# A hand-ordered attention and gated-MLP kernel: whole K copies, an earlier flag read, two separate output tiles and another order of units

## The chip, the core and the metric

The kernel runs on one core of a Trainium2 chip. A core has a matrix engine (TensorE, PE in the profile, with its weight loads shown apart as PEld), a vector engine (VectorE, DVE), a scalar engine (ScalarE, ACT), a general engine (GpSimd, POOL) and a queue engine that only issues transfers (SyncE, SP). Each engine works through its own list of instructions in order and waits on semaphores for the others. Matrix products are written to PSUM, a small memory that the vector and scalar engines read; all other data lies in SBUF. The metric is the time of one execution in microseconds of device time, and lower is better.

## The reference, cut to what matters

For 4 batches of 8 heads, 768 positions and head width 64, the kernel computes an attention within blocks whose keys and values are first mixed over the 8 blocks by a matrix P, and then a gated MLP with a mixing over positions:

```python
P = sort_net                                   # [4, 8, 8, 8]
for _ in range(5):
    P = exp(P - max(P, -1))
    P = P / (sum(P, -1) + 1e-9)
    P = P / (sum(P, -2) + 1e-9)
k_sorted = einsum('bhij,bhjcd->bhicd', P, k_b)  # blocks of 96 positions
v_sorted = einsum('bhij,bhjcd->bhicd', P, v_b)
attn = softmax(q_b @ k_sorted^T / 8)            # within each block
x = (attn @ v_sorted) as [4, 768, 512]

h = maximum(x @ w_in, 0); u, v = halves of h    # 512 each
v_n = (v - mean(v)) / sqrt(var(v) + 1e-6)
v_s = einsum('ts,bsd->btd', w_spatial, v_n) + b_spatial
out = (u * v_s) @ w_out                         # [4, 768, 512], float32
```

## The kernel before, in words

The whole program is a hand-written list of units, the string `ORDER` (lines 18 to 48). A loop at line 692 reads it word by word and calls the function of that name (`SC:1:0:3:0` calls `u_SC(1, 0, 3, 0)`), which emits its instructions on its engines. The place of a word is therefore the place of its instructions in the list of every engine that it uses. A tile framework adds the waits that the data need. A unit's first number, where it has products, is one of four PSUM tiles (`ps_tile`, line 102), each of two banks; a letter A, D or P names the engine that copies (ACT, DVE or POOL). The framework lets two engines read one PSUM tile only one after the other.

Start. `S0` loads the sort net on SP's queue, `SK:0` to `SK:4` (line 223) are five rounds of normalisation, each with one exponential on ACT and six small operations on DVE; they leave P transposed. `MC` (line 210) makes a spread identity, `MA` and `MB` a mask; `DM` (line 216) are products on zeros that keep PE busy meanwhile. `PR` multiplies P and the spread identity into PSUM. `P0` (line 260) multiplies mask and that PSUM tile into the mixing matrices of batch 0, on DVE, two heads at a time. `PC` (line 269) copies P from PSUM to SBUF, and `PD` (line 272) makes the mixing matrices of the later batches from the copy, on POOL.

Loads. All inputs but the sort net and the bias `b_bc` are loaded on POOL's queue by `L` (line 156), converted to bfloat16 in flight. They land one after the other in the order of their words. A load waits until one of eight semaphores is free, and the tiles of q, k, v and the two halves of `w_spatial` share eight buffers. `BI` (line 187) loads the bias, spread over 128 partitions, on SP's queue.

Attention, by batch, pair of heads `hp` and half of the blocks `ih`. `QT` and `QQ` transpose q for one or two pairs. `KT` (line 370) mixes and transposes k and copies the result to SBUF; the helper `natural` (line 292) splits that copy between engines when its engine word has two letters (`DA`, `AD`: the first half on the first engine). `VT` and `VB` do the same for v of batch 0; for later batches `VM` mixes v into `vm` and `VC` (line 400) moves it to `vb` by eight copies on SP's queue. `SC` (line 414) multiplies scores, with an exponential on ACT into one of five `ex` tiles; `AT` (line 459) multiplies by v, with a reciprocal and a product on DVE. `XT` transposes the result by products; batches 2 and 3 use `XD` (line 482), two DMA transposes on SP's queue.

MLP, by batch. `VP` multiplies and rectifies the v half (one or two row tiles of 128); `ST`, `LN` and `LA` are its LayerNorm on DVE and ACT; `UP` makes the u half. `WT` transposes `w_spatial` once. `SP` (line 564) mixes positions with 12 products and adds the bias on DVE into `z`, of which there are two buffers; `GT` multiplies by u, on DVE or POOL. `OP` (line 588) multiplies by `w_out` for two row tiles of 128 rows into the two banks of one PSUM tile; with two more numbers it does only some of the four terms of the sum. `OE` (line 602) copies to `o_sb`, of which there are two buffers, and `OS` (line 608) stores on SP's queue; with two more numbers they take one of the two row tiles.

Range check. The main path leaves out the maxima of the reference. `CK` (line 617) tests on DVE whether the sums that were met are in range, `CF` adds the marks with one small product, and `LF` (line 638) reads the flag into a register of every engine; after the list a branch (line 696) goes to `general_path` if it is set. It isn't set with these inputs. In the list before, `CK` stands behind batch 3's last gating product, and `CF:2 LF` are the last words.

The last words before, from the last mixing on, are:

```
SP:3:3:3 OP:1:3:0:0:3 GT:D:3:3
OP:0:3:4:0:3 OP:-1:3:0:3:4 OE:A:3:0:1:2 OP:3:3:2:0:3 CK OS:2:4 OP:-1:3:2:3:4 OE:D:3:2:1:2 OE:A:3:0:0:1 OP:-1:3:4:3:4
OS:3:0:1:2 OS:3:0:0:1 OE:A:3:2:0:1 OS:3:2:0:1 OS:3:2:1:2 OE:A:3:4:0:1 OS:3:4:0:1 OE:A:3:4:1:2 OS:3:4:1:2 CF:2 LF
```

Of the kernel before, what the change touches and what calls it, by code (L numbers as in the profile page):

```python
# [15 lines left out]


ORDER = """
S0 CO SK:0 L:q:0:0:8 L:k:0:0:8 L:v:0:0:8 L:v:1:0:8 BH SK:1 SK:2 L:k:1:0:8 ID IV:2 MC IV:0 DM:1:6:512 L:q:1:0:8 SK:3
L:wv MA DM:3:6:512 DM:1:6:512 DM:2:6:512 SK:4 L:wsb QT:1:A:0:0 MB QT:0:D:0:1 QT:3:A:0:2 DM:2:6:512 PR:3 DM:2:6:512  # L20
P0:0:2 KT:1:A:0:0 P0:6:8 L:wu P0:4:6 PC:D P0:2:4 PD:1:0:4 QT:0:D:0:3 L:wsa IV:1 PD:1:4:8 KT:2:DA:0:1 KT:3:DA:0:3
SC:1:0:0:0 SC:0:0:1:1 KT:2:D:0:2 SC:3:0:0:1 L:q:2:0:8 VT:1:D:0:0 SC:0:0:2:0 L:k:2:0:8 VT:2:D:0:1 SC:3:0:3:1 VB:1:D:0:0
VT:0:A:0:2 VB:2:D:0:1 VT:3:A:0:3 AT:1:0:0:1 VB:0:A:0:2 L:v:2:0:8 AT:2:0:0:0 L:wo VB:3:D:0:3 PD:3:0:4 SC:1:0:3:0
AT:0:0:1:1 SC:2:0:1:0 SC:3:0:2:1 AT:1:0:3:1 VM:2:A:1:0 AT:0:0:1:0 VM:3:A:1:1 AT:1:0:2:1 VM:2:A:1:2 XT:0:D:0:1:0
KT:3:A:1:2 AT:1:0:2:0 KT:0:A:1:0 AT:2:0:3:0 XT:3:A:0:1:2 KT:0:A:1:3 QQ:1:D:1:0 VM:2:A:1:3 XT:0:D:0:0:2 XT:3:D:0:0:0
SC:1:1:0:0 QQ:2:D:1:2 VC:1:0:4 KT:0:A:1:1 VP:1:D:0:0:1 SC:3:1:2:1 ST:0:0 SC:0:1:3:1 VP:2:A:0:4:5 WT:3:A:5 WT:1:D:4
VP:0:A:0:3 ST:0:5 PD:2:0:4 SC:2:1:1:0 ST:0:3 SC:1:1:2:0 UP:3:A:0:1:0 VP:2:A:0:2 VC:1:4:8 ST:0:1 ST:0:4 AT:0:1:0:0
ST:0:2 WT:1:A:3 SC:3:1:3:0 LN:0:0:6 UP:2:A:0:0:1 AT:0:1:2:0 AT:1:1:3:0 LA:0:0 PD:2:4:8 UP:3:A:0:1:1 WT:0:D:0 LA:0:2
LA:0:1 LA:0:4 AT:2:1:2:1 LA:0:3 XT:1:A:1:0:2 LA:0:5 L:v:3:0:8 WT:3:A:1 UP:0:A:0:0:0 WT:3:D:2 BI SC:1:1:0:1 QQ:2:A:2:2
AT:3:1:1:0 AT:0:1:3:1 SP:1:0:3 SC:2:1:1:1 XT:0:D:1:1:2 XT:3:A:1:0:0 AT:1:1:0:1 AT:2:1:1:1 SP:0:0:2 XT:2:A:1:1:0  # L30
GT:P:0:3 KT:1:AD:2:3 KT:3:AD:2:2 KT:0:DA:2:0 KT:2:A:2:1 GT:P:0:2 QQ:1:A:2:0 SC:0:2:3:0 VM:3:D:2:3 SP:2:0:1 VM:1:A:2:2
VM:0:A:2:1 VP:3:D:1:0:1 VM:2:A:2:0 SP:1:0:0 SC:0:2:2:1 SC:2:2:1:1 GT:P:0:1 VC:2:4:8 VC:2:0:4 ST:1:1 VP:3:A:1:4:5
SC:1:2:1:0 SC:0:2:3:1 GT:P:0:0 UP:2:A:1:0:0 PD:3:4:8 ST:1:0 ST:1:4 VP:3:D:1:2:3 VM:2:A:3:3 VM:1:A:3:0 OP:0:0:2 ST:1:2
OE:A:0:2 L:k:3:0:8 AT:1:2:3:1 VM:2:A:3:2 UP:3:A:1:1:0 ST:1:5 AT:0:2:2:1 ST:1:3 VM:2:D:3:1 L:q:3:0:8 UP:1:A:1:0:1
AT:3:2:1:1 LN:1:0:6 UP:0:A:1:1:1 LA:1:1 AT:1:2:3:0 OP:2:0:0 LA:1:0 SC:1:2:0:1 SC:0:2:2:0 OP:3:0:4 LA:1:5 OS:0:2
OE:D:0:0 LA:1:3 LA:1:4 LA:1:2 AT:2:2:0:1 AT:0:2:2:0 SP:1:1:0 OE:A:0:4 XD:2:1 SC:2:2:0:0 KT:0:DA:3:2 QQ:3:D:3:2
KT:1:D:3:1 KT:2:AD:3:0 SP:0:1:2 KT:2:A:3:3 OS:0:4 GT:D:1:0 QQ:1:A:3:0 AT:3:2:1:0 AT:0:2:0:0 VP:2:D:2:4:5 VC:3:0:4
VC:3:4:8 SC:3:3:3:0 SC:1:3:3:1 ST:2:4 XD:2:0 SP:0:1:1 SC:2:3:2:1 GT:D:1:2 SC:1:3:1:1 SP:3:1:3 AT:0:3:3:0 GT:P:1:3
AT:2:3:3:1 VP:1:A:2:2:3 ST:2:5 VP:0:A:2:0:1 OS:0:0 AT:1:3:2:1 GT:P:1:1 ST:2:3 UP:2:D:2:0:1 OP:1:1:2 SC:3:3:0:0
OE:D:1:2 ST:2:2 SC:2:3:1:0 UP:0:A:2:1:0 SC:1:3:0:1 ST:2:1 ST:2:0 LN:2:0:6 SC:3:3:2:0 UP:2:D:2:0:0 AT:0:3:1:1 LA:2:5  # L40
LA:2:4 LA:2:2 OS:1:2 UP:1:A:2:1:1 OP:2:1:0 AT:1:3:0:0 OE:A:1:0 LA:2:0 LA:2:3 LA:2:1 OP:3:1:4 AT:2:3:1:0 AT:0:3:2:0
SP:1:2:1 XD:3:0 AT:2:3:0:1 XD:3:1 GT:D:2:1 OE:A:1:4 SP:0:2:0 SP:1:2:3 GT:D:2:0 SP:0:2:2 OS:1:4 UP:3:D:3:0:0 OS:1:0
VP:0:D:3:2:3 GT:D:2:2 VP:1:A:3:0:1 ST:3:3 GT:D:2:3 ST:3:2 UP:3:A:3:0:1 VP:0:A:3:4:5 ST:3:1 OP:3:2:2 ST:3:0 OP:2:2:0
ST:3:5 ST:3:4 OE:A:2:2 LN:3:0:6 UP:1:A:3:1:1 LA:3:1 UP:0:A:3:1:0 LA:3:5 LA:3:3 LA:3:0 LA:3:2 OE:A:2:0 LA:3:4 SP:1:3:2
SP:3:3:0 GT:P:3:2 SP:0:3:1 OP:2:2:4 GT:D:3:1 OS:2:0 OS:2:2 OE:A:2:4 GT:D:3:0 SP:3:3:3 OP:1:3:0:0:3 GT:D:3:3
OP:0:3:4:0:3 OP:-1:3:0:3:4 OE:A:3:0:1:2 OP:3:3:2:0:3 CK OS:2:4 OP:-1:3:2:3:4 OE:D:3:2:1:2 OE:A:3:0:0:1 OP:-1:3:4:3:4
OS:3:0:1:2 OS:3:0:0:1 OE:A:3:2:0:1 OS:3:2:0:1 OS:3:2:1:2 OE:A:3:4:0:1 OS:3:4:0:1 OE:A:3:4:1:2 OS:3:4:1:2 CF:2 LF
"""


# [12 lines left out]
def kernel(  # L63
# [38 lines left out]
    def ps_tile(n, dt=FP32):  # L102
        return psum.tile([128, 2, 512 if dt == FP32 else 1024], dt, name=f"ps{n}", tag=f"ps{n}")

    def copy(eng, out, in_):
        if eng == "A":
            nc.scalar.copy(out=out, in_=in_)  # L107
        else:
            nc.vector.tensor_copy(out=out, in_=in_)
# [616 lines left out]
```

## Time and profile before

| What | Value |
|---|---|
| Runs, median (lowest to highest), 3 runs | 164.16 us (163.69 to 164.30) |
| Profiled execution, its own time | 163.99 us |
| Profiled execution, span on the core | 162.20 us |
| Mean granted TensorE clock | 0.988 |
| First K product | 13.17 us |
| End of the last output product | 152.98 us |
| HBM read, written | 24.78 MB, 6.29 MB |

Times inside the execution count from the start of the span. The profile's page gives each engine's busy time with its share of the span, then the span in 40 slices with the busy share in tenths, the transfer queues, the chain of waits that ended last, and the costliest groups of instructions. The trace can also be asked for a stretch of time: busy time by engine, a timeline, or what a group waited for. A transfer's time to landing runs from the start of its issue to the update of its semaphore.

The costliest groups of the computing engines, from the page: 192 products of 128x384 for the mixing over positions (33.2 us), 128 for the u half (23.3), 89 recorded of 96 of 128x512 for the v half (22.2) and 93 recorded of 96 for the output (22.0); on ACT the 32 exponentials (24.4); on DVE the 32 products of the attention (22.0), the LayerNorm's statistics (16.2) and the bias additions (15.3).

### The profile page before, as it was taken

What the parts mean: (1) busy time and instruction counts of PE and PEld (TensorE: products, weight loads), DVE (VectorE), ACT (ScalarE), POOL (GpSimd) and SP (SyncE); (2) the same over time, 40 slices, a digit from 0 to 9 for tenths busy, and PEclk for the clock granted to TensorE, in tenths of its full rate; (3) what the DMA queues carried; (4) which work ended last, traced back from release to release, by engine and by line L of the source; (5) the groups of instructions that cost most, each with busy time, mean ns of one, the idle gap of its engine ahead of it and who ended that gap; (6) DMA issues with size and microseconds to landing.
All of it is one profiled execution on the core that took longest, in us unless ns stands there. A gap on an engine that the chain in (4) does not pass through costs nothing.

```text
span 162.2 us, 3967 instructions
## 1 busy us (share of the span) xinstructions
PE 147.9 (91%) x1646; PEld 89.5 (55%) x1657; DVE 117.7 (73%) x265; ACT 84.3 (52%) x118; POOL 33.7 (21%) x39
## 2 busy tenths in 40 slices
PE   6988999899999979999999999999999999999700
...
DMA  2999999999999990479985996002059200243370
GB/s 12 191 204 205 203 205 205 210 220 237 271 206 204 206 172 0 69 133 148 184 188 94 225 149 195 0 36 97 0 107 237 113 0 0 91 172 129 129 250 25
DMA packets 27351, 23.20 MB, mean 143 GB/s; under 512 B 7232, under 2 KB 24128, under 8 KB 27328
## 3 DMA queue, kind: packets, MB, share of 16 engines
...
HBM read 24.78 MB, written 6.29 MB: 192 GB/s over the span
## 4 chain that ended last, share of the span: by engine, by line
PE 78%; ACT 7%; DVE 6%; DMA 2%; issue 2%; DVEq 0%; ACTq 0%
PE ps L569 20%; PE ps L557 13%; PE ps L514 13%; PE ps L595 11%; PE ps L468 4%; PE ps L422 4%; PE ps L363 3%; PE ps L390 3%; PE ps L307 3%; ACT ex L427 2%; ACT kt L107 2%; PE ps L498 2%; DMA out_dram<-o_sb 1%; PE ps L504 1%; ACT o_sb L107 1%
## 5 line engine op out<-in xcount | busy, mean ns | idle before, releaser
L569 PE MATMUL ps<-wspT,v_sb 128*128 128x384 bf16 x192 | 33.2, 326 | 0.0
L427 ACT ACTIVATE ex<-ps 96x768 bf16<-96x768 f32 x32 | 24.4, 806 | 12.4 <-PE ps L422 12.3
L585 POOL TENSOR_TENSOR gt<-z,u_sb 128x768 bf16<-128x768 f32 x7 | 11.4, 1640 | 92.7 <-DVE z L575 42.1
L569 PEld LDWEIGHTS <-v_sb 128*128 128x128 bf16 x192 | 18.2, 98 | 11.9 <-issue 0.2
L575 DVE TENSOR_TENSOR z<-ps,b_bc 128x768 f32<-128x768 f32 x16 | 15.3, 957 | 11.6 <-PE ps L569 11.5
L557 PE MATMUL ps<-xT,w_in_sb 128*128 128x384 bf16 x128 | 23.3, 326 | 0.0
L476 DVE TENSOR_TENSOR x_sb<-ps,rec_all 96x512 bf16<-96x512 f32 x32 | 22.0, 687 | 1.1
L514 PE MATMUL ps<-w_in_sb,xT 128*128 128x512 bf16 x89 | 22.2, 379 | 0.4
L595 PE MATMUL ps<-w_out_sb,gt 128*128 128x512 bf16 x93 | 22.0, 379 | 0.2
L107 ACT COPY o_sb<-ps 128x1024 f32<-128x1024 f32 (+1 forms) x12 | 9.8, 835 | 14.8 <-PE ps L595 12.9
L531 DVE BATCH_NORM_STATS2 stats<-v_sb 128x6 f32<-128x512 bf16 x24 | 16.2, 677 | 1.0 <-ACT v_sb L113 0.9
L113 ACT ACTIVATE v_sb<-ps 128x1024 bf16<-128x1024 f32 (+1 forms) x8 | 7.4, 920 | 17.6 <-PE ps L514 17.6
L557 PEld LDWEIGHTS <-w_in_sb 128*128 128x128 bf16 x128 | 11.8, 98 | 7.6
L595 PEld LDWEIGHTS <-gt 128*128 128x128 bf16 x96 | 9.2, 98 | 10.2
L514 PEld LDWEIGHTS <-xT 128*128 128x128 bf16 x96 | 9.0, 98 | 9.6 <-DVE x_sb L476 0.2
L113 ACT ACTIVATE u_sb<-ps 128x768 bf16<-128x768 f32 x13 | 10.6, 812 | 5.1 <-PE ps L557 5.0
L107 ACT CAST kt<-ps 128x768 bf16<-128x768 f32 (+1 forms) x14 | 8.7, 641 | 7.9 <-PE ps L363 5.5
L468 PEld LDWEIGHTS <-ex 96*128 96x128 bf16 x256 | 10.5, 97 | 3.6 <-issue 0.3
L468 PE MATMUL ps<-vb,ex 96*128 96x65 bf16 x256 | 11.9, 193 | 0.1
L219 PE MATMUL ps<-warm 128*128 128x512 bf16 x35 | 9.9, 436 | 1.3 <-DVE warm L192 1.3
L422 PE MATMUL ps<-qT,kt 64*128 64x96 bf16 x256 | 9.5, 204 | 1.6 <-ACT kt L107 1.3
L422 PEld LDWEIGHTS <-kt 64*128 64x128 bf16 x256 | 6.2, 94 | 6.9 <-issue 3.8
...
## 6 DMA issues: line engine op xcount, KB each, us to landing
...
q_in<-in_q_dram POOLq DMA_DIRECT2D x4, 768.0 KB, 18.0
k_in<-in_k_dram POOLq DMA_DIRECT2D x4, 768.0 KB, 15.1
v_in<-in_v_dram POOLq DMA_DIRECT2D x4, 768.0 KB, 21.5
...
out_dram<-o_sb SPq DMA_DIRECT2D x6, 256.0 KB, 3.2
...
```

Of the source, the lines that this page charges most:

```text
L107: nc.scalar.copy(out=out, in_=in_)
L113: nc.scalar.activation(out=out, in_=in_, func=AF.Relu)
L422: nc.tensor.matmul(t[:, hh, 0:HW].rearrange("p (g x) -> p g x", g=G)[:, :, ii * TB:(ii + 1) * TB], lhsT=kT[rows, i * BLK:i * BLK + 128], r ...
L427: nc.scalar.activation(out=e_tile(b, hp, ih).rearrange("p h (x g) -> p h x g", g=G), in_=t[0:BLK, :, 0:HW].rearrange("p h (g x) -> p h x g ...
L468: nc.tensor.matmul(t[:, hh, ii * VW:ii * VW + D + 1], lhsT=e[:, c:c + 128], rhs=vb[b % 2][:, ih * NI + ii, 2 * hp + hh, 0:D + 1], start=Tr ...
L476: nc.vector.tensor_mul(out=x_sb[:, hp].rearrange("p i (h d) -> p h i d", h=2), in0=tv[:, :, :, 0:D], in1=_raw_ap(rec, 0, [rec.ap[0], [NI, ...
L514: nc.tensor.matmul(t[:, x, :], lhsT=st["xT", b][:, n // 3, kc, (n % 3) * 128:(n % 3 + 1) * 128], rhs=w_in_sb[:, kc, DH:DFF], start=(kc == ...
L531: nc.vector.bn_stats(out=stats, in_=st["v_sb", b, n])
L557: nc.tensor.matmul(t[:, x, 0:HW], lhsT=w_in_sb[:, kc, mc * 128:(mc + 1) * 128], rhs=st["xT", b][:, ih, kc, :], start=(kc == 0), stop=(kc = ...
L569: nc.tensor.matmul(t[:, x, 0:HW], lhsT=st["v_sb", b, n][:, mc * 128:(mc + 1) * 128], rhs=wspT[:, 3 * x:3 * x + 3, n, :], start=(n == 0), s ...
L575: nc.vector.tensor_add(out=z.rearrange("p (x c) -> p x c", x=2), in0=t[:, :, 0:HW], in1=b_bc.rearrange("p (x c) -> p x c", x=2),)
L595: nc.tensor.matmul(t[:, x, :], lhsT=st["gt", b, mc][:, (n0 + x) * 128:(n0 + x + 1) * 128], rhs=w_out_sb[:, mc, :], start=(mc == 0), stop=( ...
```

## The change

The list is replaced by another of the same work. Counted by word, what differs beside the order and the choice of PSUM tiles is this:

- `KT`: before, seven whole copies on ACT, two whole ones on DVE and seven split ones (four `DA`, three `AD`); after, 13 whole ones on ACT and three on DVE.
- `PC`: on DVE between the third and the fourth `P0` before; on ACT, behind all four, after.
- `CK`, `CF` and `LF`: before at the end; after, `CK` stands ahead of the last LayerNorm unit of batch 2 (`LA:2:3`), `CF` ahead of batch 2's `SP:3:2:2`, and `LF` between `UP:1:A:3:1:1` and `SP:3:2:3`.
- The last two row tiles of batch 3, numbers 4 and 5: before, one `OP` pair in one PSUM tile, copied to `o_sb`; after, each has a PSUM tile of its own (`OH`), a copy into a buffer of the `z` pool (`OI`) and a store (`OJ`).
- `BI`: second word with a transfer after; before, amid batch 1's attention.
- `MC`: before, between `SK:2` and `SK:3`; after, behind `SK:4`.
- Loads: after, `wv` stands ahead of batch 1's q, `wu` ahead of `wsb`, and batches 2 and 3 come in the order v, (wsa), k, v of 3, q, wo, k of 3, q of 3.
- Copy engines: `QQ` five on DVE and one on ACT (before three and three); `GT` ten on POOL and six on DVE (before seven and nine); `VB`, `VM`, `WT` and `XT` each one more on DVE; `VP` one more on ACT.

The start, an inner stretch with the flag, and the end of the new list, with the new functions:

```diff
+CO S0 SK:0 BI L:q:0:0:8 ID L:k:0:0:8 L:v:0:0:8 IV:0 DM:0:6:512 L:v:1:0:8 DM:3:6:512 SK:1 L:k:1:0:8 MA SK:2 SK:3 SK:4
+L:wv L:q:1:0:8 L:wu DM:0:6:512 DM:3:6:512 IV:2 DM:0:6:512 L:wsb MC QT:2:A:0:0 DM:3:6:512 PR:2 QT:0:A:0:3 MB L:v:2:0:8
+P0:6:8 P0:0:2 P0:4:6 P0:2:4 PC:A PD:1:4:8 KT:3:A:0:3 PD:1:0:4 QT:1:D:0:1 KT:0:D:0:0 KT:2:A:0:2 BH QT:1:D:0:2 L:wsa
+SC:0:0:0:0 SC:1:0:3:0 KT:2:D:0:1 L:k:2:0:8 VT:3:A:0:0 VT:0:D:0:1 SC:1:0:2:0 IV:1 SC:2:0:3:1 VB:3:D:0:0 VT:0:A:0:3
...
+VM:2:D:2:1 WT:0:D:3 LA:0:4 VM:3:A:2:3 WT:1:D:0 WT:2:A:1 VM:0:A:2:0 KT:3:A:2:2 KT:1:D:2:3 SP:2:0:3 GT:P:0:3
...
+LN:2:0:6 AT:3:3:3:1 LA:2:4 AT:0:3:0:1 LA:2:1 GT:P:1:2 UP:2:A:3:0:0 OP:1:1:2 LA:2:5 LA:2:2 LA:2:0 UP:3:A:2:0:1 CK
+OP:2:1:4 LA:2:3 XD:3:1 ST:3:1 CF:0 OE:A:1:2 OE:A:1:4 SP:3:2:2 VP:1:D:3:2:3 VP:2:A:3:4:5 ST:3:2 ST:3:0 OS:1:2 ST:3:3
+SP:3:2:1 GT:P:2:2 ST:3:4 ST:3:5 UP:1:A:3:1:1 LN:3:0:6 LF SP:3:2:3 LA:3:2 OP:1:1:0 LA:3:3 OE:A:1:0 LA:3:0 GT:D:2:1
...
+GT:D:3:2 OS:2:4 OP:1:2:2 SP:2:3:0 OE:A:2:2 OS:2:2 SP:0:3:1 OP:2:2:0 GT:P:3:0 GT:D:3:1 SP:3:3:3 OE:A:2:0 OP:0:3:0:0:3
+GT:D:3:3 OP:3:3:2:0:3 OP:-1:3:0:3:4 OS:2:0 OE:A:3:0:1:2 OE:A:3:0:0:1 OH:2:3:5:0:3 OP:-1:3:2:3:4 OE:D:3:2:0:1
+OE:A:3:2:1:2 OS:3:0:1:2 OH:-1:3:5:3:4 OH:1:3:4:0:3 OS:3:0:0:1 OH:-1:3:4:3:4 OS:3:2:0:1 OI:A:3:5 OJ:3:5 OI:A:3:4 OJ:3:4
+OS:3:2:1:2
...
+    def u_OH(ps, b, n, lo=0, hi=4):
+        b, n, lo, hi = int(b), int(n), int(lo), int(hi)
+        if lo == 0:
+            st["o1_ps", b, n] = ps_tile(ps)
+        for mc in range(lo, hi):
+            nc.tensor.matmul(
+                st["o1_ps", b, n][:, 0, :], lhsT=st["gt", b, mc][:, n * 128:(n + 1) * 128], rhs=w_out_sb[:, mc, :],
+                start=(mc == 0), stop=(mc == FC - 1),
+            )
+
+    def u_OI(eng, b, n):
+        b, n = int(b), int(n)
+        st["o1", b, n] = moe.tile([128, S], FP32, name="o1_sb", tag="z", bufs=2)
+        copy(eng, st["o1", b, n][:, 0:DM], st["o1_ps", b, n][:, 0, :])
+
+    def u_OJ(b, n):
+        b, n = int(b), int(n)
+        nc.sync.dma_start(out=out[b, n * 128:(n + 1) * 128, :], in_=st["o1", b, n][:, 0:DM])
```

More of the change, by code (lines that the diff above doesn't have):

```diff
@@ L18 @@
 ORDER = """
[L19 to L47, printed above, removed]
+CO S0 SK:0 BI L:q:0:0:8 ID L:k:0:0:8 L:v:0:0:8 IV:0 DM:0:6:512 L:v:1:0:8 DM:3:6:512 SK:1 L:k:1:0:8 MA SK:2 SK:3 SK:4
@@ new lines @@
+L:wv L:q:1:0:8 L:wu DM:0:6:512 DM:3:6:512 IV:2 DM:0:6:512 L:wsb MC QT:2:A:0:0 DM:3:6:512 PR:2 QT:0:A:0:3 MB L:v:2:0:8
+P0:6:8 P0:0:2 P0:4:6 P0:2:4 PC:A PD:1:4:8 KT:3:A:0:3 PD:1:0:4 QT:1:D:0:1 KT:0:D:0:0 KT:2:A:0:2 BH QT:1:D:0:2 L:wsa
+SC:0:0:0:0 SC:1:0:3:0 KT:2:D:0:1 L:k:2:0:8 VT:3:A:0:0 VT:0:D:0:1 SC:1:0:2:0 IV:1 SC:2:0:3:1 VB:3:D:0:0 VT:0:A:0:3
+VB:1:D:0:1 SC:2:0:1:0 AT:3:0:0:0 VB:0:D:0:3 VM:1:A:1:1 VT:2:D:0:2 SC:3:0:2:1 VM:0:D:1:3 VM:1:A:1:0 PD:2:4:8 AT:3:0:3:0
+VM:2:A:1:2 L:v:3:0:8 PD:2:0:4 VB:0:D:0:2 SC:1:0:0:1 AT:3:0:1:0 L:q:2:0:8 KT:2:A:1:3 VC:1:0:4 AT:0:0:2:1 KT:1:A:1:1
@@ new lines @@
+AT:3:0:2:0 KT:2:A:1:0 XT:0:D:0:0:0 SC:1:0:1:1 L:wo XT:3:D:0:0:2 KT:2:A:1:2 L:k:3:0:8 AT:1:0:3:1 AT:0:0:0:1
+VP:3:A:0:0:1 AT:2:0:1:1 ST:0:0 XT:0:D:0:1:2 PD:3:4:8 VP:1:A:0:2 ST:0:2 XT:3:A:0:1:0 QQ:2:D:1:2 ST:0:1 QQ:1:A:1:0
+L:q:3:0:8 VP:3:D:0:4:5 SC:2:1:3:0 SC:0:1:0:1 VP:1:D:0:3 VC:1:4:8 ST:0:5 SC:2:1:0:0 ST:0:3 SC:3:1:1:0 SC:0:1:3:1
+UP:1:A:0:0:0 PD:3:0:4 ST:0:4 AT:2:1:0:1 LN:0:0:6 UP:3:A:0:1:1 LA:0:1 AT:0:1:0:0 WT:2:A:5 WT:1:D:4 LA:0:3 AT:3:1:3:0
+LA:0:2 LA:0:0 SC:0:1:2:0 SC:2:1:1:1 UP:1:A:0:0:1 AT:0:1:1:0 AT:2:1:3:1 LA:0:5 UP:3:A:0:1:0 WT:0:D:2 VM:1:A:2:2
```

11 lines of the change are left out of this document (added).

## The prediction

> **What bounds the kernel now.** First the totals and the slices of the span: they tell which engine is full, and when.
>
> ```profile
> span 162.2 us, 3967 instructions
> PE 147.9 (91%) x1646; PEld 89.5 (55%) x1657; DVE 117.7 (73%) x265; ACT 84.3 (52%) x118; POOL 33.7 (21%) x39
> PE   6988999899999979999999999999999999999700
> DMA  2999999999999990479985996002059200243370
> ```
>
> TensorE is full from the fourth slice to the last three, and the DMA engines are full for the first 60 us. The profiled execution took 163.99 us: 162.20 of span and 1.79 around it; the median of the runs is 164.16, 0.17 above it. I sum against 163.99. Second, busy time by stretch, cut at the first K product (13.17), the last ones' end (152.98) and two points between:
>
> ```profile
> 13.17:30.00 16.83, 15.32 (x352) 12.45 (x352) 13.77 (x29) 15.15 (x21) 6.78 (x9) 1.00 1.31 206
> 30.00:62.00 32.00, 30.75 (x447) 21.04 (x448) 23.77 (x49) 23.06 (x33) 7.22 (x6) 1.00 1.17 208
> 62.00:152.98 90.98, 90.49 (x772) 51.01 (x777) 70.19 (x135) 40.50 (x54) 10.98 (x8) 1.00 0.50 108
> 152.98:162.20 9.22, 0.09 (x1) 0.00 (x1) 0.55 (x3) 1.66 (x3) 0.00 (x0) 0.79 0.43 151
> ```
>
> Columns: length, busy PE, PEld, DVE, ACT, POOL, granted clock, DMA share, GB/s. From 62 on PE idles 0.5 of 91 us: a new order can win nothing there, only lose. Up to 62 it idles 2.8. After the last product 9.2 us pass with hardly a computation. So there are two places: the stage under the loads, and the tail. Third, the loads, since they say when the first stage may go on (issue, then time to landing):
>
> ```profile
> 21.60 0.88 POOL L162 DMA_DIRECT2D k_in<-in_k_dram  x1 [3.71 <-PE ps L381]
> ```
> ```profile
> k_in<-in_k_dram POOLq DMA_DIRECT2D x1, 768.0 KB, 29.4
> ```
> ```profile
> b_bc<-in_moe_b_spatial_dram SPq DMA_DIRECT2D x1, 384.0 KB, 7.3
> ```
> ```profile
> 55.86 1.64 PE L363 MATMUL ps<-pd,k_in 128*64 128x128 bf16 x48
> ```
>
> Batch 2's K lands at 21.60 + 29.4 = 51.0 and is first used at 55.86: now no product waits for it. Fourth, the tail:
>
> ```profile
> 150.85 1.07 ACT L107 COPY o_sb<-ps 128x512 f32<-128x512 f32 x2 [3.91 <-PE ps L595]
> 153.36 0.59 ACT L107 COPY o_sb<-ps 128x512 f32<-128x512 f32 x1 [1.43 <-DVE o_sb L109]
> 154.32 1.07 ACT L107 COPY o_sb<-ps 128x512 f32<-128x512 f32 x2 [0.37 <-DMA out_dram<-o_sb]
> ```
> ```profile
> out_dram<-o_sb SPq DMA_DIRECT2D x1, 256.0 KB, 4.0
> ```
> ```profile
> L639 PEldq TENSOR_LOAD <-flag x1: 490/490/490, 153.6 to 153.6; - x1
> L639 SPq TENSOR_LOAD <-flag x1: 912/912/912, 156.2 to 156.2; - x1
> ```
>
> ACT waits first for DVE, which copies the other half of the same PSUM tile, then for a store to land, because o_sb has two buffers and the last pair of tiles needs a third. The last copy ends at 155.40, the last store is issued at 155.79 and lands 4.0 later, at 159.8; 2.4 us of closing follow.
>
> **The order of units, head.** PE's work is the same but for order; I price it by unhindered pieces of the chain of waits: twelve K or V products 0.46, twelve Q transposes 0.335, SC 0.28, AT 0.24, XT, WT and VM 0.33 to 0.34, VB 0.58, UP 1.30, SP 1.95, VP and OP 1.73. The spread copy (L210, 0.41) leaves its place beside an exponential, where it was hidden, and follows the last Sinkhorn round, so the mask products begin at 12.2 instead of 11.9. But PE now has only one Q unit, no warm-up, between P and the first K products; these need the first mask product (12.2 + 0.36) and batch 0's K (2.32 + 10.3 = 12.6). First K at 12.7 instead of 13.17: 0.47 won. This is covered by what follows, as loads decide next.
>
> **P behind the mask products, K copies whole.** ACT's copy of P waits for DVE's fourth product (13.65), ends near 14.1, and the K copies queue behind it on ACT; the split copies took 0.48 to 0.55 a half, whole ones take 0.80 on ACT or 0.95 on DVE. First scores start near 15.2 instead of 14.63. The pair costs up to 0.6 there, and buys balance: up to some 12 us of PE work past the first K, ACT's rows sum to 12.9 instead of 14.1 and DVE's to 13.0 instead of 14.9. ACT was 10.28 busy of 11.00 from 20 to 31, so this relief is real. I book nothing for it, since K of batch 1 (4.92 + 20.0 = 24.9) and the loads after it pace PE in any case. POOL's mask products for batch 1 start 0.7 later and are not needed before 24.9.
>
> **The loads.** Before K of batch 2, the new queue carries the same bytes as the old (V of batch 2 in place of its Q, both 768 KB). b_bc moves from 38.44 to the start. In the old run 3712 KB of loads landed between 28.7 and 51.0; at 3.84 us per 768 KB (Q of batch 1 after K: 28.74 less 24.90) alone they take 18.6, so the 1176 KB of vb copies (8 x 99) and b_bc beside them cost 3.7, b_bc's third 1.2. In front it meets idle engines (12 GB/s in the first slice, 4 us) once the sort net has landed; I leave 0.2 of it. If nothing is hidden, nothing is won. So K of batch 2 lands at 50.0 (49.8 to 51.0). The new order puts 33.6 us of PE work between the first K product and this unit (96 K and 48 V products 5.5; Q 2.0; SC 4.2; VB 2.3; AT 3.1; VM 2.6; XT 1.3; VP 5.2; UP 5.2; WT 2.0): 12.7 + 33.6 = 46.3. PE therefore waits for K even after losing 3.7 us elsewhere; that is where the head's gain goes. Behind it stand 101.65 us of products. The old run spent 97.12 on 95.94 us of products from 55.86 to 152.98, 1.2 over; of these 0.9 are idle rows beside split K copies (0.29 and 0.58), which go. I take 0.8 over: 50.0 + 101.65 + 0.8 = 152.45, **0.5 won**; bounds 1.2 won to 0.9 lost, from 49.8 with 0.3 over to 51.0 with 1.2 over.
>
> **The flag.** Checks (DVE, 1.8 us), sum and flag move among products of batches 2 and 3, where DVE is 77% busy; uncovered they would delay one LayerNorm unit and its SP by 1.8. The flag is long written when read. On SP the read leaves the tail, but the branch there ended at 157.6 and the last store lands at 159.8: nothing won. On PE it now stands before SP:3:2:3, in front of 28 us of products: 0.49 + 0.11 to the next step = 0.6 if nothing covers it, 0 if PE has products queued. The nearest row for how far its sequencer runs ahead:
>
> ```profile
> L390 PEldq EVENT_SEMAPHORE  x2: 51/51/51, 23.5 to 70.1; - x2
> ```
> ```profile
> 72.39 0.81 PE L390 MATMUL ps<-v_in,pd 128*128 128x384 bf16 x4
> ```
>
> Its wait at 70.1 stands 2.3 us ahead of the products that it is for. I take **0.1 lost**. [...]
>
> **DMA transposes.** Batch 3's first is issued after its last AT, or when UP of batch 1 frees the buffer, some 5 us ahead of the VP that reads it; the old ones landed 4.6 to 5.5 after issue. 0 to 0.5, **0.1 lost**.
>
> **The tail.** Let E be the products' end. The pair 3:2 is complete 5 products, 1.08, before E. DVE copies (0.69), ACT follows (0.59) to E + 0.3, then both separate tiles at 0.535 each, with no store to wait for: last copy E + 1.37, against E + 2.42 now. SP issues store 5, store 4 and the last half of 3:2 at E + 0.85, 1.39 and 1.87, against E + 2.81 now. **0.95 won**; 0.4 if four stores near together drain at their present 0.6 spacing, 1.6 if the last lands in the 3.2 of the page's median.
>
> Sum: 163.99 - 0.5 + 0.1 + 0.1 - 0.95 = 162.74, say **162.7** (span 160.9).
>
> **Rivals.** *Loads earlier or less lost* (0.17): K at 49.8, 0.3 over, flag covered, tail 1.3: 163.99 - 1.2 - 1.3 = 161.5. For it: better balance of ACT and DVE; against: tight PSUM reuse, four tiles in both orders. *The loads take it back* (0.22): b_bc costs in front what it cost at 44, K at 51.0, 1.2 over, 0.9 lost; tail 0.95 won, flag 0.1: 164.0, or 163.5 with 0.8 over. For it: the loads fill all 60 us; against: the idle first slice. *DVE becomes the bound, slower* (0.13): until the first SP, DVE must do everything up to LA:0:4. Its rows sum to 34.6; in the old run rows of 33 were 28.9 busy (they overlap), so 30.3. From 13.65, SP may start 1.3 before LA:0:4 ends (that is its ninth product). Loads let it start at 50.9, so DVE decides below 78.5% use and the whole is slower below 76%; the old run's DVE was busy 28.89 of 36.15 there, 80%, so the margin is thin. At 74% LA:0:4 ends at 54.6, SP starts 2.4 late: 165.1. Against: part of DVE's idling came from ACT, which gets lighter. *The last tiles are not apart*: only if their z buffers were still held; those products are over 3 us earlier. Too small to count.
>
> **How the numbers follow.** Forecast 0.48, rivals 0.17, 0.22, 0.13. Less than 0.5% (0.8 us) of the median 164.16 can't be told from no change. Forecast and first rival are faster: 0.65; the second is same: 0.22; the third slower: 0.13. The range takes the first three with their bounds: 163.99 - 1.2 - 1.6 = 161.2 below, 164.0 and 0.3 for a half-covered flag = 164.3 above.
>
> **What would show it.** Right: first K near 12.7; K of batch 2 landing at 49.8 to 51.0 with PE idle before it for that load; flag loads at some 120 to 130 without a PE gap; no ACT wait for out_dram; last store issued under 2 us after the last product. Wrong: a PE gap before the first SP ended by DVE's v_sb, PE idle after 62 well over 0.5, or Q of batch 1 landing so late that its unit already stands behind.

## The result and the profile after

| | Before | After |
|---|---|---|
| Median (lowest to highest), runs side by side | 164.16 (163.69 to 164.33, 7 runs) | 165.24 (164.79 to 166.05, 7 runs) |
| Ratio to before, 95% interval | | 1.0079 [1.0054, 1.0104] |
| Profiled execution, span | 162.2 | 163.0 |
| First K product | 13.17 | 13.70 |
| Batch 2's K landed | 51.0 | 51.18 |
| End of the last output product | 152.98 | 156.16 |
| From there to the end of the span | 9.22 | 6.84 |

The kernel became slower by 0.8%, where 162.7 us and a faster kernel were forecast; 165.24 lies above the range. The last two rows of the table give the outline: the end of the program won 2.4 us, more than forecast, and the products before it ended 3.2 later.

The page of the changed kernel, totals and two rows of slices:

```profile
span 163.0 us, 3977 instructions
PE 149.1 (91%) x1657; PEld 89.5 (55%) x1657; DVE 115.9 (71%) x260; ACT 81.8 (50%) x113; POOL 38.9 (24%) x42
...
PE   6996889999999979999999988999999998999930
...
DMA  3999999999999999940260798060164003042372
```

Busy time by stretch, cut as before at the first K product, at 30 and 62, and at 155.98, just before the last product ends at 156.16 (length, busy PE, PEld, DVE, ACT, POOL, granted clock, DMA share, GB/s):

```profile
13.70:30.00 16.30, 14.74 (x328) 11.43 (x328) 12.95 (x23) 13.97 (x19) 8.96 (x10) 1.00 1.31 205
30.00:62.00 32.00, 30.53 (x440) 20.60 (x436) 25.78 (x54) 19.35 (x28) 9.79 (x9) 1.00 1.24 221
62.00:155.98 93.98, 92.33 (x835) 52.58 (x829) 68.00 (x134) 42.81 (x58) 11.45 (x7) 1.00 0.42 98
155.98:163.00 7.02, 0.18 (x1) 0.00 (x0) 0.00 (x0) 1.48 (x3) 0.00 (x0) 0.72 0.55 205
```

Behind 62 us PE idles 1.65, where it idled 0.49 before. ACT and DVE are lighter, as forecast, and neither is full in any stretch. The timeline of TensorE says where the idle time is; the bracket is the idle time ahead of a row, and what ended it:

```profile
13.70 0.53 PE L364 MATMUL ps<-pd,k_in 128*64 128x128 bf16 x12 [1.10 <-DMA k_in<-in_k_dram]
...
51.22 0.86 PE L364 MATMUL ps<-pd,k_in 128*64 128x128 bf16 x24
...
60.73 0.86 PE L308 MATMUL ps<-ident,q_in 128*64 128x128 bf16 x24 [1.06 <-DMA q_in<-in_q_dram]
...
97.24 1.90 PE L515 MATMUL ps<-w_in_sb,xT 128*128 128x512 bf16 x8 [0.50 <-DMA xT<-x_sb]
...
99.70 0.55 PE L469 MATMUL ps<-vb,ex 96*128 96x65 bf16 x13 [0.47 <-DMA vb<-vm]
...
136.54 1.46 PE L558 MATMUL ps<-xT,w_in_sb 128*128 128x384 bf16 x8 [0.62 <-DVE z L576]
```

These are the five longest waits that the timeline of the kernel before does not show, and at 51.22 K of batch 2, used as it lands: 1.1 at the first K, 1.06 for Q of batch 2, 0.5 for a DMA transpose, 0.47 for the last `vb` copy, 0.62 for a bias addition on DVE. The last one's cause stands on DVE's and POOL's timeline, 4 us earlier:

```profile
131.92 2.51 DVE L544 TENSOR_SCALAR v_sb<-v_sb,mv,rstd 128x512 bf16<-128x512 bf16 x3
...
132.31 1.64 POOL L586 TENSOR_TENSOR gt<-z,u_sb 128x768 bf16<-128x768 f32 x1 [7.18 <-PE ps L596]
```

Four of these DVE operations in a row take 1.38 us in a run below; here three take 2.51, and the line's own summary shows the one that is long (duration least/median/most in ns):

```profile
L544 DVE TENSOR_SCALAR v_sb<-v_sb,mv,rstd x24: 393/404/1868, 43.0 to 137.7; 128x512 bf16<-128x512 bf16 x24
```

In the kernel before, the same 24 took 398 to 412 ns. The bias itself, in front, landed quickly: 4.0 us from issue, at 5.2. What it did to the loads behind it is seen in the stretches from 0, in the kernel before and then after:

```profile
0.00:4.00 4.00, 2.71 (x7) 1.03 (x8) 1.69 (x19) 1.54 (x2) 2.96 (x7) 1.00 0.20 12
4.00:9.00 5.00, 4.50 (x27) 1.83 (x26) 3.88 (x19) 0.77 (x3) 4.93 (x10) 1.00 1.26 192
```
```profile
0.00:4.00 4.00, 2.72 (x7) 1.05 (x8) 1.68 (x19) 1.54 (x2) 2.87 (x9) 1.00 0.34 94
4.00:9.00 5.00, 5.00 (x22) 2.05 (x20) 3.85 (x19) 0.77 (x3) 5.00 (x8) 1.00 1.17 161
```

In the first 4 us the idle engines do take the bias (94 GB/s instead of 12). But from 4 to 9, though it is through at 5.2, 161 GB/s are moved instead of 192, and batch 0's Q lands at 9.84 instead of 8.75.

The tail, on ACT and SP, and the last stores (KB each, median us to landing):

```profile
155.90 1.56 ACT L108 COPY o_sb<-ps 128x512 f32<-128x512 f32 x3 [0.74 <-DVE o_sb L110]
157.00 0.82 SPq L635 DMA_DIRECT2D out_dram<-o_sb  x2
158.28 0.34 SPq L611 DMA_DIRECT2D out_dram<-o_sb  x1
```
```profile
out_dram<-o_sb SPq DMA_DIRECT2D x3, 256.0 KB, 2.8
```

No copy waits for a store any more. The last store is issued 2.1 behind the products instead of 2.8, lands in 2.8 instead of 4.0, and 1.9 of closing follow instead of 2.4: 0.7 + 1.2 + 0.5 = 2.4.

### The profile page after: what moved, and what is told of

It reads as the page before. It is cut to its first block, busy times and chain, and to the rows that moved or that the text cites. A ratio compares the mean times of both kernels' runs of the same rounds, so it can differ in the third digit from the quotient of the medians.

```text
span 163.0 us, 3977 instructions
## 1 busy us (share of the span) xinstructions
PE 149.1 (91%) x1657; PEld 89.5 (55%) x1657; DVE 115.9 (71%) x260; ACT 81.8 (50%) x113; POOL 38.9 (24%) x42
## 4 chain that ended last, share of the span: by engine, by line
PE 51%; DMA 32%; DVE 6%; SPq 2%; POOL 2%; ACT 2%; issue 1%; ACTq 0%; DVEq 0%; POOLq 0%
DMA q_in<-in_q_dram 19%; PE ps L570 13%; DMA v_in<-in_v_dram 11%; PE ps L596 11%; PE ps L515 8%; PE ps L558 7%; PE ps L469 3%; DVE z L576 2%; PE ps L364 2%; DMA vb<-vm 2%; PE ps L308 2%; PE ps L423 2%; SPq L404 2%; DVE v_sb L544 2%; PE ps L391 1%
## 5 line engine op out<-in xcount | busy, mean ns | idle before, releaser
L586 POOL TENSOR_TENSOR gt<-z,u_sb 128x768 bf16<-128x768 f32 x10 | 16.4, 1641 | 88.7 <-ACT ex L428 35.4
L570 PE MATMUL ps<-wspT,v_sb 128*128 128x384 bf16 x192 | 33.7, 326 | 0.0
L515 PE MATMUL ps<-w_in_sb,xT 128*128 128x512 bf16 x96 | 22.8, 380 | 0.5 <-DMA xT<-x_sb 0.5
L596 PE MATMUL ps<-w_out_sb,gt 128*128 128x512 bf16 x88 | 20.8, 380 | 0.0
L114 ACT ACTIVATE v_sb<-ps 128x1024 bf16<-128x1024 f32 (+1 forms) x9 | 8.8, 976 | 10.1 <-PE ps L515 10.1
L596 PEld LDWEIGHTS <-gt 128*128 128x128 bf16 x88 | 8.4, 98 | 9.2
L108 ACT CAST kt<-ps 128x768 bf16<-128x768 f32 x13 | 10.2, 802 | 6.4 <-PE ps L364 6.3
L476 DVE RECIPROCAL rec_all<-ps 96x8 f32<-96x8 f32 x32 | 6.2, 195 | 8.9 <-PE ps L469 8.8
L544 DVE TENSOR_SCALAR v_sb<-v_sb,mv,rstd 128x512 bf16<-128x512 bf16 x24 | 10.2, 465 | 0.1
```

Source lines behind the costliest of these rows:

```text
L114: nc.scalar.activation(out=out, in_=in_, func=AF.Relu)
L515: nc.tensor.matmul(t[:, x, :], lhsT=st["xT", b][:, n // 3, kc, (n % 3) * 128:(n % 3 + 1) * 128], rhs=w_in_sb[:, kc, DH:DFF], start=(kc == ...
L570: nc.tensor.matmul(t[:, x, 0:HW], lhsT=st["v_sb", b, n][:, mc * 128:(mc + 1) * 128], rhs=wspT[:, 3 * x:3 * x + 3, n, :], start=(n == 0), s ...
L586: eng.tensor_mul(out=gt, in0=st["z", b, mc], in1=st["u", b, mc // 2][:, mc % 2])
L596: nc.tensor.matmul(t[:, x, :], lhsT=st["gt", b, mc][:, (n0 + x) * 128:(n0 + x + 1) * 128], rhs=w_out_sb[:, mc, :], start=(mc == 0), stop=( ...
```

## The experiments

Each edit is in words of the list; nothing of the computation is left out in any of them. The kernel before was run beside each set, with medians of 163.94 to 164.08.

**1. One part undone in the changed kernel.** First the tail, with tiles 4 and 5 as one pair again:

```diff
-OH:2:3:5:0:3 ... OH:-1:3:5:3:4 OH:1:3:4:0:3 ... OI:A:3:5 OJ:3:5 OI:A:3:4 OJ:3:4
+OP:2:3:4:0:3 ... OP:-1:3:4:3:4 ... OE:A:3:4:1:2 OS:3:4:1:2 OE:A:3:4:0:1 OS:3:4:0:1
```

> The changed kernel with the last two row tiles back in one PSUM tile and in o_sb, the rest unchanged. Theory (the separate tiles shorten the closing by what the two traces differ, 9.2 to 7.0 us after the last product): the last product ends near 156.0 as in the changed kernel, a copy waits for a store again, and the time is 167.4 us. Rival (they bring only the 0.95 of the forecast, the rest of the closing is chance): 166.2 us.

Measured 167.28 (1.0204 [1.0181, 1.0228]), 2.04 more than the change. ACT waits for a store again (1.12 at 158.77). Not all of the 2.04 is the tail's: in this run batch 0's Q landed at 11.26 instead of 9.84, and the last product ended at 156.68, 0.5 later than in the changed kernel. From there to the end of the span it takes 8.60 instead of 6.84, so the tail itself brings 1.8 here.

The bias behind the loads again:

```diff
-CO S0 SK:0 BI L:q:0:0:8
+CO S0 SK:0 L:q:0:0:8
-VC:1:4:8 ST:0:5
+VC:1:4:8 BI ST:0:5
```

> The changed kernel with the bias loaded behind the value copies of batch 1, as before, instead of in front. Theory (the bias in front delays every load by 1.1 us, but Q of batch 2 sets the end of the stage and its landing has the same bytes ahead of it either way): first K product at 12.7 instead of 13.7, Q of batch 2 still landing at 60.4 to 60.8 with PE waiting for it, time 165.2 us, within 0.3. Rival (the 1.0 us at the start is carried to the end): 164.2 us.

Measured 164.78 (1.0052 [1.0025, 1.0078]), between the two. The first K product was at 12.78, close to the 12.7 of the prediction, but Q of batch 2 still landed at 60.34 and PE waited for it: what was won at the start ended in that wait, and 0.46 was left.

Q of batch 2 ahead of V of batch 3, with the bias still in front:

```diff
-L:v:3:0:8 PD:2:0:4 ... L:q:2:0:8
+L:q:2:0:8 PD:2:0:4 ... L:v:3:0:8
```

> The changed kernel with the loads of V of batch 3 and Q of batch 2 exchanged. Theory (PE's wait of 1.1 us at 60.7 is for Q of batch 2, which lands behind V of batch 3 and beside the value copies): Q lands by 57, no wait at that unit, V of batch 3 lands at 60.7 and is first used at 70, time 164.1 us. Rival (the engines behind PE were the real limit, and the wait only moves): 165.0 us.

Measured 165.86 (1.0099 [1.0068, 1.0129]), above both. The wait at `QQ:3:D:2:2` was gone (Q landed at 56.12), yet in this run batch 0's Q landed at 11.86 and the first K product stood at 15.75. The loss at the start was 3.1 us instead of 1.1, and a new wait of 1.12 stood at 69.5, where K of batch 3 lands (69.48); by its time the run decides nothing. The bias was therefore late in what follows.

The halves of `VC:3` exchanged, so that the half that is used first is copied first:

```diff
-VC:3:4:8 AT:0:2:1:1 ... VC:3:0:4 ST:2:0
+VC:3:0:4 AT:0:2:1:1 ... VC:3:4:8 ST:2:0
```

> The changed kernel with the two halves of batch 3's value copies exchanged on SP's queue, so that the half that is read first is issued ahead of the DMA transpose. Theory (PE waits 0.8 us at 99.7 for the last of four copies that queue behind the transpose): that wait goes, the 0.5 for the transpose at 97.2 stays, time 164.4 us. Rival (the copies now delay the transpose, or PE waits next for the other half): 165.2 us.

Measured 164.91 (1.0045 [1.0021, 1.007]), between the two. The wait at 99.7 was gone, that for the DMA transpose stayed. Here too Q of batch 0 came late (10.30).

**2. Is it the bias in front?** The kernel before with `BI` alone moved to the front:

```diff
-S0 CO SK:0 L:q:0:0:8
+S0 CO SK:0 BI L:q:0:0:8
-WT:3:D:2 BI SC:1:1:0:1
+WT:3:D:2 SC:1:1:0:1
```

> The kernel before, with one unit moved: the spatial bias BI goes from its place beside the loads of batch 2 to the front, ahead of the first Q. Theory (the step on the loads failed there: in front the bias costs the start what it cost later, and more, since the first Q and K queue behind its descriptors): first K product at 14.2 to 16.0 instead of 13.17, batch 2's K lands no earlier than 50.5, time 164.2 to 165.0. Rival (the step as predicted: the idle engines take it for 0.2): first K product at 13.2 to 13.4, batch 2's K lands at 50.0, time 163.2.

Measured 165.80 (1.0124 [1.0081, 1.0166]): 1.84 lost by one moved load of 384 KB (1.3 to 2.7 by the interval). First K product:

```profile
14.14 0.53 PE L363 MATMUL ps<-pd,k_in 128*64 128x128 bf16 x12
```

Batch 2's K landed at 51.24, no earlier than with the bias at 38. Its transfer alone was shorter, 28.25 from issue to landing instead of 29.45: the 1.2 that the prediction took for the bias beside it are there. But it was issued 1.39 later, at 22.99 instead of 21.60. The rival, which is the prediction's own step, falls. Over all traces, Q of batch 0 landed between 8.40 and 8.90 in the fourteen kernels without the bias in front, the one before among them, and at 9.84, 9.88, 10.30, 11.26 and 11.86 in the five with it.

**3. The waits of the new order, one after the other.** Bias late and Q of batch 2 first together:

> The changed kernel with the bias behind VC:1:4:8 again and the loads of V of batch 3 and Q of batch 2 exchanged. Theory (bias late alone won only 0.45 of its 1.1, because TensorE still waited 1.1 for Q of batch 2 at QQ:3:D:2:2): that wait is gone as well, the products end at 154.3 instead of 155.3, time 163.7. Rival (the stage ends when its bytes are through, whichever comes last): the wait reappears at V of batch 3 (VM:3:A:2:3 or so) and the time stays at 164.8.

Measured 164.31 (1.0025 [1.0015, 1.0035]). Q's wait is gone, but most of it went to the next, 0.88 at 67.7 for K of batch 3. With the halves of `VC:3` exchanged as well:

> The changed kernel with three of the four moves: bias late, V3 and Q2 exchanged, halves of VC:3 exchanged, POOL's product GT:P:2:3 still beside LA:3:1. Theory (the wait for vb, 0.8, and the wait behind the stretched LA, 0.8, count each for itself): 163.6 to 163.8, LA at 1.8 to 1.9 us, excess wait at UP:0:A:3:0:1 still there. Rival (one of the two alone made the 1.25 between them): 163.1 or 164.3.

Measured 163.57 (0.9972 [0.996, 0.9984]), as the theory had it. Then also the products `GT:P:2:1` and `GT:D:2:3` exchanged between POOL and DVE, so that POOL's stands elsewhere:

```diff
-SP:3:2:1 GT:P:2:2 ... LF SP:3:2:3 LA:3:2 ... LA:3:0 GT:D:2:1 ... LA:3:5 GT:P:2:3
+SP:3:2:1 GT:P:2:2 GT:P:2:1 ... LF SP:3:2:3 GT:D:2:3 LA:3:2 ... LA:3:0 ... LA:3:5
```

> The changed kernel with four units moved: bias late, V3 and Q2 exchanged, the halves of VC:3 exchanged, and the products GT:P:2:1 and GT:D:2:3 exchanged between POOL and DVE, so that no product of POOL runs beside LA:3:1. Theory (each wait of TensorE behind 62 us counts for itself: 0.6 for VC:3, 0.8 for the long LA): 1.4 less than without the last two moves, 162.3; LA L544 back at 0.40 us, no wait of PE for z at UP:0:A:3:0:1. [...]

Measured 163.06 (0.9951 [0.9933, 0.997]), 0.76 above the theory's time. DVE around that place, without and with this exchange:

```profile
130.72 2.38 DVE L544 TENSOR_SCALAR v_sb<-v_sb,mv,rstd 128x512 bf16<-128x512 bf16 x3
...
134.20 0.95 DVE L576 TENSOR_TENSOR z<-ps,b_bc 128x768 f32<-128x768 f32 x1
```
```profile
131.87 1.38 DVE L544 TENSOR_SCALAR v_sb<-v_sb,mv,rstd 128x512 bf16<-128x512 bf16 x4
133.61 0.96 DVE L576 TENSOR_TENSOR z<-ps,b_bc 128x768 f32<-128x768 f32 x1 [0.36 <-PE ps L570]
```

Four operations in 1.38 instead of three in 2.38, and the bias addition now waits for TensorE, not the reverse. The two moves brought 1.25 of the theory's 1.4: 0.74 for `vb`, and 0.51 for the stretched operation, which by the ratios is 0.3 with overlapping intervals, so that this second part is hardly clear of noise. Three waits remained in TensorE's row: 1.14 at 44.2, 0.87 at 67.9, 0.55 at 96.8. Moving three more units for them:

```diff
-ST:1:0 KT:2:A:3:3 SC:1:2:0:0 ... VP:3:A:1:4:5 VM:1:A:3:2
+ST:1:0 SC:1:2:0:0 ... VP:3:A:1:4:5 KT:2:A:3:3 VM:1:A:3:2
-UP:1:A:0:0:0 PD:3:0:4 ST:0:4 ... LA:0:4 VM:3:A:2:3
+UP:1:A:0:0:0 ST:0:4 ... LA:0:4 PD:3:0:4 VM:3:A:2:3
-ST:2:0 VP:2:A:2:4:5 GT:P:1:1 ... SP:0:1:3 SC:3:3:2:0
+ST:2:0 SP:0:1:3 VP:2:A:2:4:5 GT:P:1:1 ... SC:3:3:2:0
```

> The changed kernel with the four moves and three more: KT:2:A:3:3 behind VP:3:A:1:4:5, PD:3:0:4 behind LA:0:4, SP:0:1:3 ahead of VP:2:A:2:4:5. Theory (the three waits left in TensorE's row, 0.87 for K of batch 3 at 67.9, 1.14 for the stretched LA at 44.2, 0.55 for the DMA transpose at 96.8, are each a matter of place; the one at 44.2 lies ahead of batch 2's K, which lands at 51.1 whatever happens before it, so it is worth little): 163.06 - 0.87 - 0.55 - 0.1 = 161.5, products ending at 152.5. Rival (slack that the waits made is used by others, as with the bias alone): 162.4 or more.

Measured 165.37 (1.0079 [1.0063, 1.0096]): the rival, and worse. The waits at 67.9 and 96.8 were gone. The one at 44.2 stayed: POOL runs ahead in its list, and `PD` started at 41.9 as before the move. TensorE waited at new places, among them

```profile
97.57 2.11 PE L570 MATMUL ps<-wspT,v_sb 128*128 128x384 bf16 x12 [0.73 <-ACT ex L428]
...
103.51 0.51 PE L423 MATMUL ps<-qT,kt 64*128 64x96 bf16 x16 [1.62 <-DVE x_sb L477]
```

and 0.92 at 71.5 for a K copy on ACT, which now stood right ahead of the next user of its PSUM tile. The moves made other units late; that the four shared PSUM tiles are the reason is the likely reading, not tried by itself.

**4. The change's other parts, in the order of before.** The new tail alone, in the kernel before:

> The kernel before with the changed kernel's tail alone: last two output tiles apart, the flag's read still at the end. Theory (the tail is worth 2.05, as the old tail in the changed kernel cost; the flag's read hides behind the last stores): 162.1, products' end at 153.0, last store issued under 2 us later. Rival (the sum as predicted, 0.95, or the flag's read and branch now stand behind the shorter tail and take some of it): 163.0 to 163.3.

Measured 162.69 (0.9919 [0.9903, 0.9936]), 1.27 won, between the two; the last two stores took 4.4 and 4.5 to land there. With the seven split K copies made whole as well:

```diff
-KT:2:DA:0:1 KT:3:DA:0:3 ... KT:1:AD:2:3 KT:3:AD:2:2 KT:0:DA:2:0 ... KT:0:DA:3:2 ... KT:2:AD:3:0
+KT:2:D:0:1 KT:3:A:0:3 ... KT:1:D:2:3 KT:3:A:2:2 KT:0:D:2:0 ... KT:0:A:3:2 ... KT:2:A:3:0
```

> The kernel before with the changed tail, and the seven split K copies made whole, each on one engine, in the same order of units. Theory (the two waits of TensorE beside K copies, 0.69 at the first scores and 0.58 at 59.2, last only longer with whole copies of 0.8 to 0.95, for the first scores wait on the copy alone; the lighter ACT and DVE gain nothing, as loads and TensorE set the pace): 162.7 to 163.1, PE waits of 0.9 to 1.2 for kt. Rival (ACT's load under the loads was what made scores late, and whole copies relieve it): waits shorter, 162.2.

Measured 161.83 (0.986 [0.984, 0.988]), 0.86 more: the rival. TensorE beside batch 2's K, first with the split copies and then with whole ones:

```profile
57.72 0.86 PE L308 MATMUL ps<-ident,q_in 128*64 128x128 bf16 x24 [0.29 <-DVE kt L110]
59.15 0.35 PE L423 MATMUL ps<-qT,kt 64*128 64x96 bf16 x8 [0.58 <-ACT kt L108]
```
```profile
57.55 0.86 PE L308 MATMUL ps<-ident,q_in 128*64 128x128 bf16 x24
58.41 0.35 PE L423 MATMUL ps<-qT,kt 64*128 64x96 bf16 x8
```

Both waits, 0.87, are gone and nothing took their place. The converse, the repaired new order of 163.06 with split copies:

> The changed kernel with the four moves, and seven K copies split between ACT and DVE as in the kernel before. Theory (whole copies are worth nothing here, since loads set the pace up to 62 us): 162.9 to 163.3, the same. Rival (the lighter ACT and DVE are what keeps this order going): 163.8 or more.

Measured 164.09 (1.0009 [1.0, 1.0019]), 1.03 more, with two new waits for `kt` of 0.58 and 0.99. So whole copies are worth about 0.9 in either order.

The flag, first put back to the end in the repaired new order:

> The changed kernel with the four moves (bias late, V3 and Q2 exchanged, halves of VC:3 exchanged, POOL's product away from LA:3:1), and with the flag's sum and its reading put back behind the last store; the checks, memset and compares, follow the last G product. Theory (the reading amid the products is hidden behind TensorE's queue, and at the end it hides behind the last store's 2.8 us of landing): the same as without this move, 163.06, within 0.3. Rival (the reading, 0.49 on PE to 0.9 on SP plus the branch, ends behind the landing of the shorter tail): 163.5 to 164.0.

Measured 164.39 (1.002 [1.0008, 1.0032]), 1.33 more, beyond the rival. The products ended no later than with the flag among them (153.75, against 154.26), so the loss lies behind them: two stores that are issued while the engines branch, between 155.0 and 157.5, land in 4.18 and 4.44. The flag moved alone in the kernel before:

```diff
-LA:3:4 SP:1:3:2 SP:3:3:0 GT:P:3:2 SP:0:3:1 OP:2:2:4 GT:D:3:1 OS:2:0 OS:2:2 OE:A:2:4 ... CK ... CF:2 LF
+LA:3:4 CK SP:1:3:2 SP:3:3:0 CF:2 GT:P:3:2 SP:0:3:1 OP:2:2:4 LF GT:D:3:1 OS:2:0 OS:2:2 OE:A:2:4 ...
```

> The kernel before, with the flag alone moved: the checks behind LA:3:4, its sum behind SP:3:3:0, its reading behind OP:2:2:4, tail and order else as before. Theory (not the reading's own time counts: when all engines branch behind it at once, between 154 and 157, they fetch instructions, and the stores issued there land 4.0 to 4.5 later instead of 2.4 to 3.1): last stores land 2.5 to 3 after issue, time 162.5 to 162.9. Rival (the prediction's: nothing won, for the branch ends ahead of the last landing anyway): 163.9 to 164.1, landings of 4.0.

Measured 163.51 (0.9969 [0.9941, 0.9998]): landings of 2.2 to 2.3, even shorter than expected, but only half of the time, since SP's reading held back finished stores (from 140.05 to 144.37) and ACT's last copies stood at 156.00 instead of 154.32. With `LF` one place further on, behind `OE:A:2:4`:

> As the kernel before with the flag alone moved, but its reading one place further on, behind the stores OS:2:0 and OS:2:2 and the copy OE:A:2:4. Theory (where it was, SP waited for the flag until 143.4 with two finished stores queued behind it, 139.2 being their time without it; o_sb came free late, ACT's last copies stood at 156.0 instead of 154.3, and that took back most of the 1.4 won at the last landings): copies at 154.3 again, landings 2.2 to 2.8, time 162.5 to 162.8. Rival (stores that land together share the bandwidth, and the flag is worth the 0.57 seen): 163.4 to 163.6.

Measured 163.10 (0.9946 [0.9929, 0.9963]), 0.96 won, between the two: the last stores landed in 2.6 to 2.8, but ACT's last copies stood at 154.99, not at 154.3 again. The transfers around the last stores in the kernel before, and in this one:

```profile
DMA packets 554, 1.05 MB, mean 257 GB/s; under 512 B 58, under 2 KB 58, under 8 KB 549
...
q14 instruction: 4, 0.03, 2.4%
q8 instruction: 1, 0.02, 1.6%
...
out_dram<-o_sb SPq DMA_DIRECT2D x3, 256.0 KB, 4.1
```
```profile
DMA packets 578, 1.07 MB, mean 260 GB/s; under 512 B 64, under 2 KB 64, under 8 KB 576
...
q14 instruction: 2, 0.02, 0.9%
...
out_dram<-o_sb SPq DMA_DIRECT2D x4, 256.0 KB, 2.6
```

Three stores land in 4.1, four in 2.6, while the mean rate is the same: with the flag at the end a 16 KB packet of a queue that the profile names instruction (q8) lies among them, beside four of 8 KB (q14) instead of two.

**5. All three parts in the order of before.** With `LF` where SP holds stores, and behind them:

> The kernel before in its own order of units with three parts of the change: tail apart, K copies whole, flag read amid the last batch's products. Theory (the parts add: 161.83 with tail and K copies, less 1.3 for the stores that land in 2.8 instead of 4.4): 160.4 to 160.7. Rival (the checks' 1.8 on DVE or the readings delay the products near the end): 161.5 or more.

> The order of before with tail apart, whole K copies and the flag amid the last products, read behind OS:2:0, OS:2:2 and OE:A:2:4. Theory: last store issued at 153.8 again instead of 154.8, landing 2.8 later, time 160.3 to 160.7. Rival: as without this step, 161.4.

Measured 161.42 (0.9831 [0.9799, 0.9864]), the rival's time, and 160.63 (0.9789 [0.9773, 0.9806]), the theory's. The second is 3.43 faster than before and the fastest kernel found. Its stretches:

```profile
30.00:62.00 32.00, 31.74 (x457) 21.67 (x455) 24.87 (x49) 23.33 (x32) 7.11 (x6) 1.00 1.17 207
62.00:151.90 89.90, 89.84 (x775) 50.41 (x773) 69.14 (x135) 40.58 (x54) 10.98 (x8) 1.00 0.50 108
151.90:158.90 7.00, 0.38 (x2) 0.00 (x0) 0.08 (x1) 1.56 (x3) 0.00 (x0) 0.85 0.57 213
```

From 30 on TensorE idles 0.26 of 32 us under the loads and 0.06 behind. Nothing is left for an order to win there.

**What the parts are worth.** Tail 1.27, whole K copies 0.86 on top of it, flag 0.96: the sum is 3.09, and together they bring 3.43. Tail and flag help each other: from the products' end to the end of the span it takes 9.22 before, 8.13 with the tail alone, 8.20 with the flag alone, 6.66 with both. The change holds all three and is 1.08 slower than before; by the ratios, 1.0079 against 0.9789, its new order costs 2.9%, some 4.7 us, against the old order with the same parts. Four moves took back 2.1 of it (1.0079 to 0.9951). Of the other 2.7 the profiled executions show 2.0, and it is idle time of TensorE: 3.84 between the first K product and the last product's end in the repaired new order, 1.71 in the fastest kernel. The three waits that were left, 2.56, are most of the 3.84, but the one try at moving them lost time, so what the new order would need to lose them stays open.

## Why the prediction was wrong, point by point

**The sum, term by term.** The forecast's span was 160.9, the profiled execution's 163.0. Batch 2's K was used at 51.22 instead of 50.0: 1.2 more. From there to the last product's end it took 104.94, which is 3.3 over the 101.65 of products where the sum had 0.8, and 0.2 for flag and transpose: 2.3 more. The end took 6.84 instead of 9.22 - 0.95 = 8.27: 1.4 less. So two steps failed, the price of the bias in front and the "0.8 over" behind batch 2's K, and a third, the end, was better than forecast.

**The loads, the first step that failed.** "In front it meets idle engines [...] I leave 0.2 of it": the engines were idle and took the bias, but Q and K of batch 0, issued behind it, came 1.07 later (by up to 3.1 in other runs). The head's gain of 0.47 became a loss of 0.53, and batch 2's K, issued 1.17 later (at 22.77 instead of 21.60; POOL had waited 3.74 for a load of V to land), landed at 51.18, just beyond 49.8 to 51.0. The mis-sized term is the 0.2: alone in the old order the bias in front made that issue 1.39 later, more than the 1.2 won by taking it from beside the K load. The rival "the loads take it back" had the mechanism and set its price too low: moved alone, the bias cost 1.84. With the bias behind again, the first K product stood at 12.57 to 12.78 in four kernels, as the 12.7 of the sum, and at 13.15 to 13.25 in three, where the first mask product began 0.4 to 0.6 later.

**The list of the loads stopped too early.** The sum went from batch 2's K straight to "101.65 us of products". In the new order Q of batch 2 lands behind V of batch 3 and beside the eight `vb` copies, at 60.69, and its first product waited 1.06. Each load's place and its first user were at hand in the order.

**"0.8 over" behind 50 us, the second step that failed.** It measured 3.3. TensorE idled 2.71 there, and four waits are 2.65 of that; the other 0.6 is busy time over the sum's 101.65. Beside the wait for Q, two kinds of row were left out of it: `vb` copies that SP issues behind a waiting DMA transpose (with the transpose 1.0 instead of the 0.1 booked), and a DVE operation that stretches beside POOL's product (1.87 instead of 0.40, with the wait of 0.62 at 136.5 behind it). From 62 on, 1.65 of idling showed instead of 0.49, which the prediction had named as a sign of being wrong. "A new order can win nothing there, only lose" was right, and it should have been priced.

**The flag.** That the reading is covered was right: on PE it took

```profile
L659 PEldq TENSOR_LOAD <-flag x1: 485/485/485, 125.9 to 125.9; - x1
```

while the products it stands before began at 128.82, 2.4 us after it ended, without a gap. "Nothing won" was wrong: it argued from SP's branch, which ended ahead of the last landing, and not from that landing itself, which takes 4.0 to 4.5 with the flag at the end and 2.1 to 3.5 with it read early. Forecast 0.1 lost, measured 0.96 won.

**The tail.** Right in mechanism, mis-sized: 0.95 forecast, 1.27 measured alone. The copies came as forecast (the last one ended 1.30 behind the products, 1.37 in the sum), the last store 2.12 behind them instead of 1.87. What the sum did not have is the closing behind the last landing, 0.5 shorter: 1.92 in the fifteen kernels whose last store is of row tile 3, 2.43 in the four where it is of row tile 5, and no run shows why. With the flag's 0.96 the tail makes 2.2 of the 2.4 that the profile shows between the products' end and the span's end.

**Whole K copies.** "I book nothing for it", beyond the two idle rows counted in "0.8 over": measured 0.86 to 1.03. The two rows of 0.29 and 0.58 account for it. They were seen, and put into a sum of other losses instead of into a term of their own.

**The other rivals.** DVE did not become the bound: no product waited for `v_sb` and its busy time fell from 117.7 to 115.9. The last two tiles are apart, as the three copies of ACT in a row show.
